# Output group pairs of an attention and SwiGLU kernel: where the sums between the products stand, and in which order the last unit ends

## The chip, the cores and the metric

The kernel runs on one core of a Trainium2 chip. The metric is device time in microseconds (us). A core has five engines with one instruction queue each: TensorE (PE in the profile; its weight loads are listed as PEld), VectorE (DVE), ScalarE (ACT), GpSimd (POOL) and SyncE (SP), which here issues DMAs. Engines meet through semaphores. Each engine takes its own instructions in the order in which the program gives them, so the place of an instruction in that order decides what stands behind it.

## The reference, cut to what matters

```
scores = q @ k^T / sqrt(64)                  # 8 batches x 12 heads, 448 tokens, head width 64
attn   = softmax(scores);  x = attn @ v      # x as 3584 tokens x 768
g, val = x @ w_gate, x @ w_val               # 768 -> 1536
out    = (silu(g) * val) @ w_out             # 1536 -> 768, float32
```

## The kernel before, in words

Tokens are held transposed: features on the 128 partitions, tokens along the free axis. Two batches (896 tokens) make one block of X. Attention for the later heads runs interleaved with the feed-forward part of earlier blocks up to about 301 us. What follows is the tail, and all that the change touches lies in it.

**Products with seven multiplications.** In the tail a 2 x 2 block product is done with seven sub-products in place of eight (the Winograd form). That saves TensorE work and needs sums of operand blocks made ahead: sums of weights (`weight_sums`, L756 to L759, GpSimd, four per unit, called W below), sums of tokens (`token_sums`, L990 to L993, VectorE, tile T), and sums of the hidden values h (`h_sums`, L538 to L541). One call of `h_sums` gives four sums in a chain: s3 = a11 - a21, then a21 becomes a21 + a22 in place, s2 = a21 - a11, s4 = a12 - s2. Each is one instruction over 128 x 768 elements.

**Units.** `Unit` (L793 to L860) computes two feature blocks of g or val for two token halves. There are twelve units, of 256 columns from 301.9 us on (tokens 384 to 895 of the third block), and later twelve of 448 columns (the fourth block). A unit has products P1 to P7 on TensorE (three matmuls each, tiles `un` and `ub`), copies A1 and A2 on ScalarE, sums D1 (L842) and D2 (L846) on VectorE, and four results F00, F01, F10, F11. The results of even units are Silu on ScalarE (L858), those of odd units a multiplication on VectorE (L860) that writes h into `hts`. F11 (the row with `silu,kept`) reads both its operands from SBUF; the other three read one from PSUM. P7 waits for D1 of its unit, P4 for D2.

**The planner.** `order_of` takes items (engine, estimated time, predecessors), runs through them in estimated time, and so fixes the order on every engine. For the units of 256 columns the items hold, beside the units: the W sums of units 6 to 11, then the four G sums (`h_sums` on GpSimd for the first 256 tokens of the third block), four H sums (`h_sums` on VectorE for the tokens 384 to 639; H0 after unit 5, H1 to H3 after unit 11), and the step O: the last `plain_out` (L648), twelve matmuls of 192 columns, one ScalarE copy (L655) and a store of two DMAs on SP. O stands behind P2, P3 and P4 of unit 11.

**Output group pairs.** `out_group` (L677 to L733) gives 256 tokens x 384 output columns with seven products of six matmuls each (0.49 us per product). A pair is two of them, for the two column halves, and shares one set of four h sums. Within a group:

- first stage: products into a, into c (needs the sum a21), into b (needs s2). ScalarE copies a to p1 (L718), VectorE makes p15 (L719) and writes a new c (L721).
- second stage: a product into b again (needs s3); VectorE reads it with the row that the code calls `part` (L725); products into a and into c (needs s4); ScalarE copies the first row out (L696); a third product into b; VectorE reads it (L733). The third product into b may not start before `part` has read b.

`run_groups` runs a pair as: first stage of one, first stage of two, second stage of one, second stage of two. Behind each of these four it takes one instruction from the list `sums` (`add_sum`). So VectorE has four slots for sums per pair, all at the ends of stages. The hook `mid`, called between `part` and the next products, was there already, for another use. Three pairs follow the units of 256 columns (331 to 354 us), and three follow the units of 448 columns (406 us to the end). The slots of the first three hold the T sums for the next units and the h sums of the third pair; four slots are empty. The slots of the last three hold the h sums of the pair that follows.

Of the kernel before, what the change touches and what calls it, by code (L numbers as in the profile page):

```python
# [38 lines left out]
PE_, ACT_, DVE_, POOL_ = "PE", "ACT", "DVE", "POOL"  # L39
# [25 lines left out]
def kernel(  # L65
# [10 lines left out]
    nc = tc.nc  # L76
    B, H, S, D = q.shape
    DM = H * D
    DF = moe_w_gate.shape[1]
    P = 112  # L80
    NC = S // P
    NCB = DM // 128
    NFB = DF // 128
# [53 lines left out]
    NH = NFB // 2  # L137
# [6 lines left out]
    Hall = [[hsum[:, m] for m in range(3)], [hsum[:, 3]]]  # L144
# [5 lines left out]
    def hview(lo, n):  # L150
        return hall[:, ds(lo * NFB, n * NFB)].rearrange("p (f t) -> p f t", t=n)
# [378 lines left out]
            lambda: nc.vector.tensor_sub(t4, b21, t2),  # L530
        ]

    def h_sums(hts, t, at, eng=nc.vector):
        lo, hi, x, y = slice(0, NH), slice(NH, NFB), ts(2 * t, 128), ts(2 * t + 1, 128)
        a11, a12, a21, a22 = hts[:, lo, x], hts[:, hi, x], hts[:, lo, y], hts[:, hi, y]
        s2, s3, s4 = Hall[at]
        return [
            lambda: eng.tensor_sub(s3, a11, a21),  # L538
            lambda: eng.tensor_add(a21, a21, a22),
            lambda: eng.tensor_sub(s2, a21, a11),  # L540
            lambda: eng.tensor_sub(s4, a12, s2),  # L541
        ]
# [339 lines left out]
    with tc.manual_schedule():  # L882
# [48 lines left out]
        sums = []  # L931
# [3 lines left out]
        def pair_groups(kk, c0, hts, t, last=False, at=None):  # L935
            at = t if at is None else at
            osb = []

            def begin(qw, own=False, mid=None):
                if not qw:  # L940
                    osb.extend(new_osb() for _ in range(2))
                return out_group(kk, c0, hts, t, at, qw, osb, last, own, mid)

            return [(lambda own=False, mid=None, qw=qw: begin(qw, own, mid), h_sums(hts, t, at) if not qw else []) for qw in range(2)]
# [41 lines left out]
        def token_sums(x, w, t, eng=nc.vector):  # L986

            b11, b12, b21, b22 = (x[:, ts(h, NK), ts(bb, w)] for h in range(2) for bb in range(2))
            return [
                lambda: eng.tensor_sub(t[0], b12, b11),  # L990
                lambda: eng.tensor_sub(t[1], b22, t[0]),
                lambda: eng.tensor_sub(t[2], b22, b12),
                lambda: eng.tensor_sub(t[3], b21, t[1]),  # L993
            ]
# [14 lines left out]
        def add_sum(n=1):  # L1009
            for _ in range(n):  # L1010
                if sums:
                    sums.pop(0)()
# [149 lines left out]
        while g < last or queue:  # L1162
            n = 2 if g < WIDE * NC else 3
# [33 lines left out]
        for x, (chunks, todo) in enumerate(plan):  # L1197
# [54 lines left out]
            if 0 < base - x <= len(FIRST_STEPS):  # L1252
                n = FIRST_STEPS[x - base]
# [101 lines left out]
        def run_items(items):  # L1355
            items = {n: (e, t, [a for a in after if a in items], fn) for n, (e, t, after, fn) in items.items()}
            for name in order_of(items):
                items[name][3]()

        units = {}  # L1360
        items = unit_items(units, lambda u: Unit(u, 256, x5, t5, hts5), 256)
# [10 lines left out]
        for u in range(6, NFB):  # L1372
            items[f"W_{u}"] = (POOL_, 3.65, [f"W_{u - 1}"], lambda u=u: weight_sums(u))
        groups5 = [pair_groups(KL - 1, 384, hts5, t, at=1 - t) for t in range(2)]
        for m, fn in enumerate(groups5[0][0][1]):
            u = NFB - 1 if m else NH - 1
            items[f"H{m}"] = (DVE_, 0.6, [f"F00_{u}", f"F10_{u}"] + [f"H{m - 1}"] * (m > 0), fn)

        sums.clear()
        for m, fn in enumerate(h_sums(hview(0, 384), 0, 0, nc.gpsimd)):  # L1380
            items[f"G{m}"] = (POOL_, 1.85, [f"G{m - 1}" if m else f"W_{NFB - 1}"], fn)
        items["O"] = (PE_, 1.0, [f"P{n}_{NFB - 1}" for n in (2, 3, 4)], run_o)
        run_items(items)

        def run_groups(pairs):
            for pair in pairs:
                gens = [begin() for begin, _ in pair]
                for stage in range(2):
                    for gen in gens:
                        next(gen)  # L1390
                        add_sum()

        x7 = X[KL]
        t7 = token_space(xp.tile([128, NCB, NT], FP16, tag="X", name="T")[:].rearrange("p a b -> p (a b)"), S)
        tsums7 = token_sums(x7, S, t7)
        behind = groups5[1][0][1]
        rest = lambda: None
        sums.extend([tsums7[0], rest, rest, behind[0], behind[1], behind[2], tsums7[1], behind[3]])
        sums.extend([tsums7[2], rest, rest, tsums7[3]])
        for pair in [groups] + groups5:  # L1400
            run_groups([pair])

        hts = hview(0, NT)
        units = {}
        items = unit_items(units, lambda u: Unit(u, S, x7, t7, hts), S)
# [14 lines left out]
        for m, fn in enumerate(final[0][0][1]):  # L1420
            u = NFB - 1 if m else NH - 1
            items[f"H{m}"] = (DVE_, 0.65, [f"F00_{u}", f"F10_{u}"] + [f"H{m - 1}"] * (m > 0), fn)
        run_items(items)

        sums.extend(f for pair in final[1:] for _, fs in pair for f in fs)
        run_groups(final)


# [28 lines left out]
```

## Time and profile before

| | |
|---|---|
| median of 3 runs | 433.75 us (433.72 to 433.98) |
| profiled execution, its own time | 433.57 us |
| its span in the profile | 431.8 us |
| PE busy | 422.4 us (98%) |
| DVE, ACT, POOL busy | 270.3, 245.5, 233.6 us |
| granted TensorE clock, mean | 0.999 |

The span is counted from the first to the last instruction of the trace; the profiled execution's own time is 1.8 us more. A line of the timeline has the start (us from the start of the span), the duration, the engine, the line of the kernel, the operation, written tile <- read tiles, shape and count. In square brackets stands idle time of that engine before it, and what ended it. Matmuls are pipelined and their ends are modelled: six matmuls of 192 columns show 0.66 us, but the next six start 0.49 us after them. So a stop of TensorE is read from the starts, not from the idle time in the brackets.

### The profile page before, as it was taken

What the parts mean: (1) busy time and instruction counts of PE and PEld (TensorE: products, weight loads), DVE (VectorE), ACT (ScalarE), POOL (GpSimd) and SP (SyncE); (2) the same over time, 40 slices, a digit from 0 to 9 for tenths busy, and PEclk for the clock granted to TensorE, in tenths of its full rate; (3) what the DMA queues carried; (4) which work ended last, traced back from release to release, by engine and by line L of the source; (5) the groups of instructions that cost most, each with busy time, mean ns of one, the idle gap of its engine ahead of it and who ended that gap; (6) DMA issues with size and microseconds to landing.
All of it is one profiled execution on the core that took longest, in us unless ns stands there. A gap on an engine that the chain in (4) does not pass through costs nothing.

```text
span 431.8 us, 11525 instructions
## 1 busy us (share of the span) xinstructions
PE 422.4 (98%) x4594; PEld 286.4 (66%) x4594; DVE 270.3 (63%) x635; ACT 245.5 (57%) x395; POOL 233.6 (54%) x354
## 2 busy tenths in 40 slices
PE   8999999999999999999999999999999999999995
PEld 3666656554557677747665677777888985555795
DVE  4666562775668655575535776677778655565662
ACT  6975667546655655656666546668564225545221
POOL 8756633998877775638744785936997000000001
PEclk9999999999999999999999999999999999999999
DMA  9999999999999999999988998923100231000124
GB/s 141 177 199 200 199 172 182 137 144 226 159 126 138 132 175 124 140 117 133 113 151 127 134 138 109 150 58 84 21 2 25 89 98 49 2 0 2 37 75 147
DMA packets 108550, 50.01 MB, mean 116 GB/s; under 512 B 60864, under 2 KB 105232, under 8 KB 108496
## 3 DMA queue, kind: packets, MB, share of 16 engines
q0 software_dynamic: 46944, 24.83, 52.0%
q1 hardware_dynamic: 61408, 24.27, 32.1%
q8 instruction: 36, 0.59, 0.6%
q10 hardware_dynamic: 144, 0.17, 0.1%
q14 instruction: 18, 0.15, 0.1%
HBM read 49.55 MB, written 11.01 MB: 140 GB/s over the span
## 4 chain that ended last, share of the span: by engine, by line
PE 84%; DVE 7%; DMA 3%; ACT 3%; issue 1%; POOL 1%; SPq 0%; DVEq 0%; POOLq 0%
PE og L677 16%; PE gp L555 15%; PE vp L555 12%; PE un L793 9%; PE acc L418 7%; PE ub L793 7%; PE s L327 4%; PE op L648 3%; PE s L357 2%; PE acc L383 2%; DVE hts L614 2%; DMA qkT<-qk 1%; PE tp L300 1%; DVE t L608 1%; ACT E L347 1%
## 5 line engine op out<-in xcount | busy, mean ns | idle before, releaser
L347 ACT ACTIVATE E<-s 128x896 f16<-128x896 f32 x126 | 106.6, 918 | 40.5 <-PE s L327 28.4
L237 POOL COPY qk<-qkraw 128x512 f16<-128x512 f16 x72 | 44.5, 659 | 55.8 <-DMA qkT<-qk 54.4
L555 PE MATMUL gp<-X,wg 128*128 128x384 f16 (+1 forms) x360 | 73.9, 347 | 0.0
L555 PE MATMUL vp<-X,wv 128*128 128x384 f16 (+3 forms) x360 | 70.1, 332 | 0.2
L608 DVE SCALAR_TENSOR_TENSOR t<-sg,gp 128x384 f32<-128x384 f32 (+1 forms) x60 | 36.3, 607 | 41.6 <-ACT sg L582 41.5
L555 PEld LDWEIGHTS <-wv 128*128 128x128 f16 x420 | 40.3, 98 | 28.1 <-issue 0.6
L638 POOL DMA_DIRECT2D out_dram<-osb x3 | 1.6, 541 | 93.7 <-ACT osb L696 93.7
L555 PEld LDWEIGHTS <-wg 128*128 128x128 f16 x360 | 32.8, 98 | 26.1 <-issue 1.9
L177 POOL DMA_DIRECT2D vraw<-in_v_dram x72 | 43.9, 631 | 9.4 <-DVE t L608 7.1
L582 ACT ACTIVATE sg<-gp 128x384 f32<-128x384 f32 (+1 forms) x60 | 32.1, 537 | 29.2 <-PE gp L555 28.4
L418 PEld LDWEIGHTS <-E 128*128 128x128 f16 (+1 forms) x1152 | 37.3, 96 | 13.1 <-issue 6.8
L177 POOL DMA_DIRECT2D qkraw<-in_k_dram x70 | 42.3, 616 | 6.6 <-DMA wo<-in_moe_w_out_dram 5.3
L677 PEld LDWEIGHTS <-hts 128*128 128x128 f16 x528 | 44.1, 98 | 1.6 <-issue 1.3
L365 ACT ACTIVATE E<-s 112x896 f16<-112x896 f32 x48 | 40.4, 925 | 8.1 <-PE s L357 7.8
L418 PE MATMUL acc<-vo,E 128*128 128x65 f16 (+1 forms) x1152 | 43.3, 193 | 1.4 <-DVE hts L614 0.4
L614 DVE SCALAR_TENSOR_TENSOR hts<-t,vp 128x384 f16<-128x384 f32 (+3 forms) x60 | 34.1, 568 | 7.2 <-PE vp L555 3.3
L696 ACT ACTIVATE osb<-og 128x384 f32<-128x384 f32 x22 | 10.8, 491 | 40.9 <-PE og L677 32.9
L200 POOL DMA_DIRECT2D qkraw<-in_q_dram x44 | 29.8, 678 | 5.7 <-DMA vraw<-in_v_dram 1.4
L448 DVE TENSOR_TENSOR xt<-acc,R 128x256 f16<-128x256 f32 x72 | 30.6, 424 | 2.5
L327 PE MATMUL s<-qkT 64*128 64x448 f16 x216 | 29.6, 353 | 0.0
L677 PE MATMUL og<-wo,hts 128*128 128x192 f16 x264 | 29.0, 246 | 0.0
L677 PEld LDWEIGHTS <-hsum 128*128 128x128 f16 x300 | 25.4, 98 | 1.6 <-DVE og L721 0.6
(180 smaller groups left out, 719.0 us busy)
## 6 DMA issues: line engine op xcount, KB each, us to landing
vraw<-in_v_dram POOLq DMA_DIRECT2D x72, 64.0 KB, 4.8
qkraw<-in_q_dram POOLq DMA_DIRECT2D x41, 112.0 KB, 4.2
qkraw<-in_k_dram POOLq DMA_DIRECT2D x68, 64.0 KB, 4.7
wg<-in_moe_w_gate_dram POOLq DMA_DIRECT2D x8, 288.0 KB, 9.9
wv<-in_moe_w_val_dram POOLq DMA_DIRECT2D x8, 288.0 KB, 10.2
wo<-in_moe_w_out_dram POOLq DMA_DIRECT2D x2, 1152.0 KB, 19.4
out_dram<-osb SPq DMA_DIRECT2D x7, 288.0 KB, 3.6
out_dram<-osb SPq DMA_DIRECT2D x6, 336.0 KB, 3.5
```

The source lines that it names most:

```text
L177: eng.dma_start(dst[ts(s, 64)], rows)
L237: nc.gpsimd.tensor_copy(dst.rearrange("p c h d -> p h c d"), src)
L327: nc.tensor.matmul(s[:, hx, 0:S], lhsT=t[ts(hx, 64), ts(c + low(pr, hx), 128)], rhs=t[ts(hx, 64), ds(NC * 128, S)], start=True, stop=True,)
L347: nc.scalar.activation(e[:, 0 : 2 * S].rearrange("p (h q) -> p h q", h=2), s[:, :, 0:S], AF.Exp, scale=sm_scale)
L365: nc.scalar.activation(e[:, :, 0:S], s[0:P, :, 0:S], AF.Exp, scale=sm_scale)
L418: nc.tensor.matmul(acc[:, ts(j, D + 1)], lhsT=e[rows, ds(hx * S + j * 128, 128)], rhs=Vts[pr % NV][rows, hx, col, 0 : D + 1], start=first, ...
L555: nc.tensor.matmul(dst[:, 0:w], lhsT=wslice(kind, self.fb, cb), rhs=X[kk][:, cb, ds(c0 + lo, w)], start=(cb == 0), stop=(cb == NCB - 1),)
L582: self.readers = [nc.scalar.activation(self.sg[:, 0:n], gp[:, 0:n], AF.Tanh, scale=0.5)]
L608: nc.vector.scalar_tensor_tensor(self.t1[:, 0:n], self.sg[:, 0:n], 1.0, self.gp[:, 0:n], ALU.add, ALU.mult)
L614: nc.vector.scalar_tensor_tensor(self.hts[:, self.fb, ds(lo, w)], self.t1[:, ds(lo, w)], 0.5 * HS, vp[:, 0:w], ALU.mult, ALU.mult)
L677: nc.tensor.matmul(dst, lhsT=lhs(n), rhs=rhs(n), start=first and n == 0, stop=n == NH - 1, skip_group_check=True)
L793: mm = nc.tensor.matmul(dst, lhsT=lhs[:, n], rhs=rhs[:, n], start=first and n == 0, stop=n == NK - 1, skip_group_check=True,)
```

## The change

1. **Slots.** `run_groups` keeps one sum behind the first stage of group one and one behind the whole pair. The two others move into the middle of the second stages (`mid`), between `part` and the last VectorE instruction of the group.
2. **G in halves.** The four GpSimd sums become eight of half the width (three of the six blocks each, 128 x 384), in turn for the two halves.
3. **H behind the units.** The four H sums leave the planner's items. The first is issued straight behind the units, the three others take the next slots. The empty slots are gone; the list is now: T sum 1, H1 to H3 (first pair), the four h sums of the third pair (second pair), T sums 2 to 4 (third pair).
4. **O ahead of P4.** O now stands behind P2, P3 and P7 of unit 11, and P4 of unit 11 behind O.

`run_groups` also runs the last three pairs, so part 1 holds there too.

```
-    def h_sums(hts, t, at, eng=nc.vector):
-        lo, hi, x, y = slice(0, NH), slice(NH, NFB), ts(2 * t, 128), ts(2 * t + 1, 128)
+    def h_sums(hts, t, at, eng=nc.vector, f0=0, n=NH):
+        lo, hi, x, y = ds(f0, n), ds(NH + f0, n), ts(2 * t, 128), ts(2 * t + 1, 128)
         a11, a12, a21, a22 = hts[:, lo, x], hts[:, hi, x], hts[:, lo, y], hts[:, hi, y]
-        s2, s3, s4 = Hall[at]
+        s2, s3, s4 = (h[:, lo] for h in Hall[at])
...
         groups5 = [pair_groups(KL - 1, 384, hts5, t, at=1 - t) for t in range(2)]
-        for m, fn in enumerate(groups5[0][0][1]):
-            u = NFB - 1 if m else NH - 1
-            items[f"H{m}"] = (DVE_, 0.6, [f"F00_{u}", f"F10_{u}"] + [f"H{m - 1}"] * (m > 0), fn)
-
         sums.clear()
-        for m, fn in enumerate(h_sums(hview(0, 384), 0, 0, nc.gpsimd)):
-            items[f"G{m}"] = (POOL_, 1.85, [f"G{m - 1}" if m else f"W_{NFB - 1}"], fn)
-        items["O"] = (PE_, 1.0, [f"P{n}_{NFB - 1}" for n in (2, 3, 4)], run_o)
+        halves = [h_sums(hview(0, 384), 0, 0, nc.gpsimd, f0, NH // 2) for f0 in (0, NH // 2)]
+        for m, fn in enumerate(fn for both in zip(*halves) for fn in both):
+            items[f"G{m}"] = (POOL_, 0.95, [f"G{m - 1}" if m else f"W_{NFB - 1}"], fn)
+        items["O"] = (PE_, 1.0, [f"P{n}_{NFB - 1}" for n in (2, 3, 7)], run_o)
+        items[f"P4_{NFB - 1}"][2].append("O")
         run_items(items)
 
         def run_groups(pairs):
             for pair in pairs:
-                gens = [begin() for begin, _ in pair]
-                for stage in range(2):
-                    for gen in gens:
-                        next(gen)
-                        add_sum()
+                one, two = (begin(mid=add_sum) for begin, _ in pair)
+                next(one)
+                add_sum()
+                for gen in (two, one, two):
+                    next(gen)
+                add_sum()
...
-        behind = groups5[1][0][1]
-        rest = lambda: None
-        sums.extend([tsums7[0], rest, rest, behind[0], behind[1], behind[2], tsums7[1], behind[3]])
-        sums.extend([tsums7[2], rest, rest, tsums7[3]])
+        first, behind = (pair[0][1] for pair in groups5)
+        first[0]()
+        sums.extend([tsums7[0], *first[1:], *behind, *tsums7[1:]])
```

## The prediction

> **What bounds the kernel now.** I read the page first: shares, then the slices.
>
> ```profile
> PE 422.4 (98%) x4594; PEld 286.4 (66%) x4594; DVE 270.3 (63%) x635; ACT 245.5 (57%) x395; POOL 233.6 (54%) x354
> ```
>
> TensorE is the bound and no product is removed, so the change can only win where TensorE stands still. I took the timeline of all engines from 296 us to the end and compared the starts of successive PE rows. Undisturbed, three matmuls of 256 columns take 0.33 us from start to start, six of 192 columns 0.49. Stops of 0.08 us that recur once per two units are left aside. Every larger one, by engine:
>
> ```profile
> 317.89 1.13 DVE L538 TENSOR_TENSOR qkraw<-hts 128x768 f16<-128x768 f16 x1
> 318.81 0.49 PE L793 MATMUL ub<-vraw,E 128*128 128x256 f16 x3
> 318.95 0.41 DVE L846 TENSOR_TENSOR kept<-ub,kept 128x256 f32<-128x256 f32 x1
> 319.41 0.49 PE L793 MATMUL ub<-vraw,wg 128*128 128x256 f16 x3
> ...
> 325.28 1.64 POOL L538 TENSOR_TENSOR hsum<-hts 128x768 f16<-128x768 f16 x1
> 325.82 1.38 DVE L860 SCALAR_TENSOR_TENSOR hts<-silu,kept 128x256 f16<-128x256 f32 x1
> 327.41 0.49 PE L793 MATMUL un<-vraw,vo 128*128 128x256 f16 x3
> 328.26 0.49 PE L793 MATMUL ub<-vraw,wsum 128*128 128x256 f16 x3 [0.36 <-DVE un L842]
> ...
> 330.32 0.49 PE L793 MATMUL un<-X,vo 128*128 128x256 f16 x3
> 331.00 0.49 PE L793 MATMUL ub<-vraw,wv 128*128 128x256 f16 x3 [0.19 <-DVE kept L846]
> 331.05 1.37 DVE L860 SCALAR_TENSOR_TENSOR hts<-silu,kept 128x256 f16<-128x256 f32 x1
> 334.30 0.56 DVE L541 TENSOR_TENSOR qkraw<-hts,hsum 128x768 f16<-128x768 f16 x1
> 334.78 0.35 DVE L719 SCALAR_TENSOR_TENSOR p<-og,p 128x192 f32<-128x192 f32 x1
> 334.79 0.66 PE L677 MATMUL og<-E,hsum 128*128 128x192 f16 x6
> 335.65 0.67 PE L677 MATMUL og<-E,hsum 128*128 128x192 f16 x6 [0.21 <-DVE og L721]
> ```
>
> Read from the starts: P4 of unit 6 is 0.27 late (319.41 - 318.81 - 0.33), behind D2, which stood behind H0. P7 of unit 10 is 0.52 late, behind D1, which stood behind F11 of unit 9. P4 of unit 11 is 0.35 late, behind its own D2. The second stage of the first pair is 0.37 late (335.65 - 334.79 - 0.49): p15 could start only when H3 was through, though ScalarE had p1 ready at 333.83.
>
> The same timeline has the second kind of stop, the third product into b behind `part`:
>
> ```profile
> 343.64 0.55 DVE L540 TENSOR_TENSOR hsum<-hts 128x768 f16<-128x768 f16 x1
> 343.83 0.66 PE L677 MATMUL og<-wo,qkraw 128*128 128x192 f16 x6
> 344.11 0.35 DVE L725 SCALAR_TENSOR_TENSOR osb<-og,p 128x192 f32<-128x192 f32 x1
> 344.51 0.66 PE L677 MATMUL og<-qkraw,hts 128*128 128x192 f16 x6
> ```
>
> A sum goes ahead of `part`; the product starts 0.19 late. By the same reading it is 0.27 late at 346.76, 0.19 at 410.77 and 0.19 at 417.88; in the first pair, where the slot is empty, 0.26 at 337.40, since all of VectorE's work there is late. The third and sixth pair, whose slots there are empty, have no such stop. All nine: 0.27 + 0.52 + 0.35 + 0.37 + 0.26 + 0.19 + 0.27 + 0.19 + 0.19 = 2.61 us.
>
> **H sums behind the units (part 3).** H0 leaves its place at 317.89. D2 of unit 6 then starts when P7 (start 318.15, record 0.49) is through, about 318.66, and ends by 319.08; P4 may start at 319.14 undisturbed. Saved: 0.27. H1 to H3 (three rows of 0.56) leave the stretch ahead of the first p15, and H0 comes there; worked out below.
>
> **G in halves (part 2).** F11 of unit 9 took 1.38 us; its fellows that read PSUM take 0.41. It ended (327.20) 0.28 after the GpSimd sum that ran beside it (326.92). F11 of unit 11 shows the same: end 332.42, GpSimd row to 332.14. So this instruction waits for the GpSimd instruction that is running. A half has the form of the W rows, 128x384, 0.91 us. F11 of unit 9 moves to 325.55 (0.27 earlier), the first half runs from about 325.1 to 326.0, so F11 ends near 326.3 and not 327.2. F01 and F10 follow at 0.34 each, D1 ends near 327.3; P7 of unit 10 is due at 327.47. Saved: 0.52. Bounds: everything if the half ends early, and nothing lost below zero, since a shorter neighbour cannot hold F11 longer; the upper end of its wait is one half plus 0.28, 1.19 us, which still meets P7. GpSimd pays: eight times 0.91 and two extensions of 0.18 (the W rows that run into an F11 show 1.09) give 7.6 us where four took 6.86. It ends near 333.0, not 332.14. Its cover is slack: s2 (sixth half, about 331) is read at 332.2 by the new count, s4 (eighth) at 335.2.
>
> **O ahead of P4 (part 4).** By the planner's rule the order of TensorE changes in this alone. After P3 of unit 11 come the 0.99 us of O, and D2 (0.42) is done inside them. Saved: 0.35. What moves with O: twelve weight loads, the ScalarE copy (0.33; ScalarE was idle 2.34 us before it) and two store DMAs on SP, whose queue is empty from 307 us on. O's bank is that of unit 10, last read at 330.18 minus the 0.79 saved so far: 329.39, before O's start at 329.86. P4 itself comes 0.99 behind its old place in the order, and F10 on VectorE waits for it: P4 ends near 331.35, and F01, which stands ahead of F10, near 331.55, so F10 does not wait.
>
> **The first pair.** TensorE starts it at 332.31 - (0.27 + 0.52 + 0.35) = 331.17. F10 of unit 11 ends near 331.9; the H sum behind it (0.56, up to 1.13 beside GpSimd, as H0 shows) ends between 332.4 and 333.0. The nearest row is H0's: I take 332.5 to 333.0. p1 is ready 1.52 after the pair's start (333.83 - 332.31), 332.7. So p15 starts at 332.75 to 333.0. Before, p15 at 334.78 led through c, T sum 1, the second p15 and c to `part` ending at 337.35, 2.57 later. Now `part` ends at 335.3 to 335.6; the product behind it is due at 331.17 + 9 x 0.494 = 335.62. Both stops (0.37 and 0.26) close, the second with as little as nothing to spare.
>
> **The slots (part 1).** In the second pair `part` starts where the sum stood (343.64) and ends at 344.0, before the 344.33 at which the product is due; likewise for the second group. Saved: 0.19 + 0.27, and 0.19 + 0.19 in the last pairs. Each moved sum now lies between `part` and the last row of the group. That row waits for the third product (0.8 to 1.2 us idle before it on VectorE in all pairs), so a sum of 0.56 or a T sum of 0.86 fits. H2 and H3 of the first pair are read by the second pair's products about 1.4 and 3 us after they end; T sum 2 ends near 348 and is read by P6 at 353.8.
>
> **The sum.** Nothing else is added to TensorE. 433.57 (profiled execution) - 2.61 = 430.96. The median stands 0.18 over that execution, so 431.15 for a median.
>
> One page is weighed. The Trainium skill, SBUF — State Buffer, section Who interferes with whom, says that a VectorE instruction with two SBUF inputs and a GpSimd instruction that reads SBUF exclude each other for a whole instruction, whichever came first. By the rows of F11 the trace agrees, but for about 0.13 us: the second one ends 0.28 after the first and takes 0.41 alone. By that rule H0 in its new place, and no longer after the end of GpSimd's work, is the part that speaks against the change; the rival below prices it.
>
> **The rivals.**
> *Part of the gain only.* H0, now behind the units, meets the last halves. If it waits for the eighth and not the seventh, it ends near 333.4, p15 starts at 333.4, `part` ends at 335.95: 0.3 is kept as a stop, and up to all 0.63 if GpSimd runs later still. For it: H0 took 1.13 at 317.89. Against: VectorE got in after one GpSimd instruction each time. Another source: the chain of waits puts T sum 1 behind a store of O (2.27 us). No idle stands before it on VectorE, so I do not believe it, but if true it waits until 334.1 and costs 0.33. With the 0.63, the 0.33, and 0.3 for F11 beside a half that starts late: 433.75 - 2.61 + 1.26 = 432.4; the middle of this case is 431.9.
> *Slower: the middle sums hold up the products.* They stand in program order ahead of three products. If these waited for the sum, each of two second stages would lose about 1.1 us (344.0 + 0.55 against a product due at 343.34), in five pairs 11 us: 442. It decides from 0.35 us per stage, ten stages, on. Against: an in-place h sum at 409.90 stood ahead of the products at 409.59 and 410.09, and neither waited.
> *No gain: a half costs as much as a whole.* At 1.64 per half s2 would end at 334.9, 2.7 later than its reader at 332.2: 433.75 - 2.61 + 2.7 = 433.8. Against: 0.90 to 0.92 in the undisturbed W rows of that shape. It decides from about 1.1 us per half.
>
> **How the numbers follow.** All nine stops close: 0.60, range 430.7 to 431.6 (the runs shown lie within 0.3). Part of the gain: 0.28, up to 432.6. Middle sums in the way, or any other new wait on that side: 0.07. Halves too dear, within 0.2%: 0.05. 0.2% (0.87 us) is about what a measurement of this kernel can tell from no change. Faster 0.88, same 0.05, slower 0.07. The time is that of the first case, 431.15; the range 430.6 to 432.5 takes in most of the second.
>
> **What would show it.** After: P4 of unit 6 0.33 after the product ahead of it; F11 of unit 9 at 0.5 to 0.9 us; O's rows ahead of the last `ub` rows with no wait; p15 of the first pair started by p1 and not by a sum; `part` in the second, fourth and fifth pair at once behind its product, and six-matmul rows 0.49 apart to the end. The prediction is wrong if a PE row in 331 to 354 us waits for a sum on either engine, or if units 6 to 11 show new stops of D1 or D2.

## The result, and the profile after

The changed kernel takes 430.93 us (median of 6 runs, 430.33 to 431.62), the kernel before 433.87 us (6 runs, 433.57 to 434.66): a ratio of 0.9929, 95% interval 0.9914 to 0.9944. The forecast was 431.15.

The page after, first rows:

```profile
span 429.7 us, 11530 instructions
...
PE 421.5 (98%) x4594; PEld 286.6 (67%) x4594; DVE 267.5 (62%) x635; ACT 245.4 (57%) x395; POOL 234.1 (54%) x358
```

The same 4594 matmuls, and GpSimd has four instructions more (the halves). The shares tell nothing; where the time went has to be read from the starts of the PE rows. This is the timeline of the changed kernel, from the first product of the units to the second pair:

```profile
302.20 0.49 PE L793 MATMUL un<-X,wg 128*128 128x256 f16 x3
...
319.15 0.49 PE L793 MATMUL ub<-vraw,E 128*128 128x256 f16 x3
319.50 0.49 PE L793 MATMUL ub<-vraw,wg 128*128 128x256 f16 x3
...
325.41 1.97 POOL L538 TENSOR_TENSOR hsum<-hts 128x384 f16<-128x384 f16 x2
325.99 0.61 DVE L860 SCALAR_TENSOR_TENSOR hts<-silu,kept 128x256 f16<-128x256 f32 x1
327.57 0.49 PE L793 MATMUL un<-vraw,vo 128*128 128x256 f16 x3
327.90 0.49 PE L793 MATMUL ub<-vraw,wsum 128*128 128x256 f16 x3
...
329.96 0.49 PE L793 MATMUL un<-X,vo 128*128 128x256 f16 x3
330.29 1.15 PE L648 MATMUL op<-wo,hts 128*128 128x192 f16 x12
330.81 1.97 POOL L541 TENSOR_TENSOR hsum<-hts,hsum 128x384 f16<-128x384 f16 x2
331.28 0.49 PE L793 MATMUL ub<-vraw,wv 128*128 128x256 f16 x3
331.61 0.66 PE L677 MATMUL og<-wo,hts 128*128 128x192 f16 x6
331.88 0.42 DVE L860 SCALAR_TENSOR_TENSOR hts<-silu,ub 128x256 f16<-128x256 f32 x1 [0.41 <-ACT osb L655]
332.27 0.92 DVE L538 TENSOR_TENSOR qkraw<-hts 128x768 f16<-128x768 f16 x1
332.80 0.33 ACT L718 ACTIVATE p<-og 128x192 f32<-128x192 f32 x1 [0.99 <-PE og L677]
333.16 0.36 DVE L719 SCALAR_TENSOR_TENSOR p<-og,p 128x192 f32<-128x192 f32 x1
333.90 0.85 DVE L990 TENSOR_TENSOR T<-X 128x1344 f16<-128x1344 f16 x1
335.39 0.35 DVE L725 SCALAR_TENSOR_TENSOR osb<-og,p 128x192 f32<-128x192 f32 x1
335.57 0.66 PE L677 MATMUL og<-wo,hsum 128*128 128x192 f16 x6
336.06 0.66 PE L677 MATMUL og<-qkraw,hts 128*128 128x192 f16 x6
...
342.31 0.35 DVE L725 SCALAR_TENSOR_TENSOR osb<-og,p 128x192 f32<-128x192 f32 x1
342.50 0.66 PE L677 MATMUL og<-wo,qkraw 128*128 128x192 f16 x6
342.58 0.55 DVE L539 TENSOR_TENSOR hts<-hts 128x768 f16<-128x768 f16 x1
342.99 0.66 PE L677 MATMUL og<-qkraw,hts 128*128 128x192 f16 x6
...
424.64 0.66 PE L677 MATMUL og<-qkraw,hts 128*128 128x192 f16 x6
```

What to see: P4 of unit 6 starts 0.35 after the product ahead of it (0.60 before), P7 of unit 10 0.33 after (0.85 before), O follows P3 without a stop and P4 follows O (330.29 + 0.99 = 331.28). In the first pair p15 (333.16) starts 0.03 after p1 is ready (333.13), the same distance as in the trace of parts 1 and 3 together, where VectorE had been waiting for p1 (333.99 and 334.02). The H sum ahead of it has its end at 333.19; rows of VectorE that follow each other without a wait overlap by up to 0.08 (before: H3 to 334.86, p15 from 334.78). So p1 was the last to come, by about 0.05. `part` ends at 335.74, 0.32 before the product that needs b free. In the second pair the in-place sum (342.58) stands behind `part`, and the six-matmul rows are 0.49 apart. None of the nine stops is left.

The whole time is a coarse measure for single parts of the change, since the stretch ahead of the units, which no kernel here changes, ended anywhere from 301.38 to 303.16 us in the traces. So I use the length of the **tail**: from the start of the first product of the 256-column units to the start of the last product of the last pair. It is cut at the first product of the first pair, of the 448-column units, and of the fourth pair. No part changes the 448-column units, and they take 51.94 or 51.95 in all fourteen traces, so differences of a few hundredths of a microsecond can be read from one trace of each kernel:

| trace | units | pairs 1 to 3 | 448-column units | pairs 4 to 6 | tail |
|---|---|---|---|---|---|
| before | 30.45 | 21.87 | 51.95 | 20.66 | 124.93 |
| changed | 29.41 | 20.79 | 51.95 | 20.29 | 122.44 |
| difference | -1.04 | -1.08 | 0.00 | -0.37 | -2.49 |

The two medians differ by 2.94. The 0.45 more would then lie ahead of the units, where the runs scatter; that is worked out, not shown, because only one run of each kernel left a trace. In the experiments with several runs the medians differ from those of the kernel before by between 0.57 less and 0.08 more than the tails do, so 0.45 is of the size of the scatter. In these two traces the units start 0.34 later in the changed kernel, and the two profiled executions are 2.14 apart (433.57 and 431.43): 2.49 less 0.34.

### The profile page after: what moved, and what is told of

The parts are those of the page before. It is cut to its first block, busy times and chain, and to the rows that moved or that the text cites. A ratio compares the mean times of both kernels' runs of the same rounds, so it can differ in the third digit from the quotient of the medians.

```text
span 429.7 us, 11530 instructions
## 1 busy us (share of the span) xinstructions
PE 421.5 (98%) x4594; PEld 286.6 (67%) x4594; DVE 267.5 (62%) x635; ACT 245.4 (57%) x395; POOL 234.1 (54%) x358
## 4 chain that ended last, share of the span: by engine, by line
PE 79%; DMA 12%; DVE 4%; ACT 2%; issue 1%; POOL 0%; SPq 0%; DVEq 0%
PE og L677 17%; PE gp L555 13%; PE un L793 10%; PE vp L555 10%; PE acc L418 8%; PE ub L793 8%; DMA qkraw<-in_k_dram 5%; PE s L327 4%; PE op L648 3%; DMA wv<-in_moe_w_val_dram 3%; DMA vraw<-in_v_dram 3%; PE s L357 2%; DVE hts L614 2%; PE acc L383 1%; ACT E L347 1%
```

## The experiments

Two theories stood against each other. **Stops add up**: each part is worth the stops that it closes, alone or with the others. **Stops are linked**: TensorE must not only come earlier, the instruction it waits for must come earlier as well, and a part that speeds up one side only moves the stop. Each part was made alone on the kernel before, and undone alone in the changed kernel. The measure is the tail.

| kernel | units | pairs 1 to 3 | pairs 4 to 6 | tail | against its base |
|---|---|---|---|---|---|
| before + slots (1) | 30.42 | 21.41 | 20.30 | 124.07 | -0.86 |
| before + halves (2) | 29.91 | 21.77 | 20.67 | 124.30 | -0.63 |
| before + H behind (3) | 30.23 | 21.99 | 20.67 | 124.84 | -0.09 |
| before + O ahead (4) | 30.08 | 22.21 | 20.67 | 124.91 | -0.02 |
| changed without slots | 29.43 | 21.99 | 20.67 | 124.04 | +1.60 |
| changed without halves | 29.85 | 20.79 | 20.30 | 122.89 | +0.45 |
| changed without H behind | 29.57 | 21.71 | 20.30 | 123.52 | +1.08 |
| changed without O ahead | 29.77 | 20.79 | 20.30 | 122.81 | +0.37 |
| before + 1 + 3 | 30.22 | 20.79 | 20.29 | 123.25 | -1.68 |
| before + 2 + 4 | 29.57 | 22.14 | 20.67 | 124.33 | -0.60 |

The four parts alone add to 1.60, the four undone to 3.50, all together give 2.49. So the parts are linked, and the rows show where.

### Slots alone

```
 kernel before, run_groups
-    gens = [begin() for begin, _ in pair]
-    for stage in range(2):
-        for gen in gens:
-            next(gen)
-            add_sum()
+    one, two = (begin(mid=add_sum) for begin, _ in pair)
+    next(one)
+    add_sum()
+    for gen in (two, one, two):
+        next(gen)
+    add_sum()
```

> The kernel before with part 1 alone (two of four sums in the middle of the second stages; the old list, G whole, H in the planner's items, O behind P4). The tail is the time from the start of the first product of the 256-column units to the start of the last product of the last pair: 124.93 before, 122.44 after. Both theories: the stops of 0.19 and 0.27 in the second pair and of 0.19 each in the fourth and fifth pair close, those of the first pair stay: 124.93 - 0.84 = 124.1. If sums in the middle held up products, the tail would be longer than before.

Measured: 124.07; time ratio to the kernel before 0.9986 (0.9975 to 0.9998). The stops of the second, fourth and fifth pair are gone, those of the first pair stand (0.36 and 0.27). Sums in the middle of the second stages cost nothing, so the rival that they hold up products falls.

### Halves alone

```
 kernel before
-    for m, fn in enumerate(h_sums(hview(0, 384), 0, 0, nc.gpsimd)):
-        items[f"G{m}"] = (POOL_, 1.85, ...)
+    halves = [h_sums(hview(0, 384), 0, 0, nc.gpsimd, f0, NH // 2) for f0 in (0, NH // 2)]
+    for m, fn in enumerate(fn for both in zip(*halves) for fn in both):
+        items[f"G{m}"] = (POOL_, 0.95, ...)
```

> The kernel before with part 2 alone (G in halves). Additive theory: only P7 of unit 10 comes on time, 0.52 less: tail 124.4. Theory of linked stops: F11 of unit 11 waits for a half too and not for a whole, so H1 to H3 end 0.6 to 1.2 earlier, and the 0.37 and 0.26 of the first pair shrink or close as well: tail 123.8 to 124.1.

Measured: 124.30; ratio 0.9983 (0.9971 to 0.9995). Here the theory of linked stops named a number that was too low, and the additive one (124.4) came nearer. P7 of unit 10 is on time and F11 of unit 11 takes 0.47, as it said. But H1, which follows, then meets the eighth half. VectorE and GpSimd in the timeline of this kernel:

```profile
330.60 0.47 DVE L860 SCALAR_TENSOR_TENSOR hts<-silu,kept 128x256 f16<-128x256 f32 x1
330.99 0.41 DVE L860 SCALAR_TENSOR_TENSOR hts<-silu,un 128x256 f16<-128x256 f32 x1
331.50 0.42 DVE L860 SCALAR_TENSOR_TENSOR hts<-silu,ub 128x256 f16<-128x256 f32 x1
331.95 1.17 DVE L539 TENSOR_TENSOR hts<-hts 128x768 f16<-128x768 f16 x1
...
334.22 0.35 DVE L719 SCALAR_TENSOR_TENSOR p<-og,p 128x192 f32<-128x192 f32 x1
```

```profile
330.74 1.96 POOL L541 TENSOR_TENSOR hsum<-hts,hsum 128x384 f16<-128x384 f16 x2
```

H1 ends at 333.12, 0.42 after the last half (332.70). Counted from the start of the units (301.95 here, 301.86 before), the first p15 comes 0.65 earlier than before and the pair itself 0.54 earlier, so its two stops stay (0.27 and 0.26, against 0.37 and 0.26). Most of the wait that F11 lost came back at H1.

### H behind the units, alone

```
 kernel before
-    for m, fn in enumerate(groups5[0][0][1]):
-        u = NFB - 1 if m else NH - 1
-        items[f"H{m}"] = (DVE_, 0.6, ...)
...
-    sums.extend([tsums7[0], rest, rest, behind[0], behind[1], behind[2], tsums7[1], behind[3]])
-    sums.extend([tsums7[2], rest, rest, tsums7[3]])
+    first, behind = (pair[0][1] for pair in groups5)
+    first[0]()
+    sums.extend([tsums7[0], *first[1:], *behind, *tsums7[1:]])
```

> The kernel before with part 3 alone: H behind the units and the new list of sums, but all slots at the ends of stages. Additive theory: H0's 0.27 and the first pair's 0.37 and 0.26 close: tail 124.0. Theory of linked stops: H0 is worth 0.2, the 0.37 closes, but every slot now holds a sum ahead of the row that frees b: a stop of about 0.2 in the first pair, 0.2 in the second, 0.5 and 0.25 behind T sums in the third. Tail 124.9 to 125.2, no gain.

Measured: 124.84; ratio 0.9996 (0.9985 to 1.0007). The 0.37 of the first pair closes, the units are 0.22 shorter, and all of it is given back in the pairs: stops of 0.20, 0.20, 0.60 and 0.24, since the list now has a sum for every slot and half of the slots stand ahead of `part`. P7 of unit 10 is 0.46 late here, not 0.52.

### O ahead of P4, alone

```
 kernel before
-    items["O"] = (PE_, 1.0, [f"P{n}_{NFB - 1}" for n in (2, 3, 4)], run_o)
+    items["O"] = (PE_, 1.0, [f"P{n}_{NFB - 1}" for n in (2, 3, 7)], run_o)
+    items[f"P4_{NFB - 1}"][2].append("O")
```

> The kernel before with part 4 alone (O ahead of P4 of unit 11). Additive theory: 0.35 less, tail 124.6. Theory of linked stops: the first pair starts 0.35 earlier, but H1 to H3 end when they did, so its second stage waits 0.35 longer: units 0.35 shorter, the three pairs 0.35 longer, tail 124.9.

Measured: 124.91; ratio 1.0004 (0.9990 to 1.0018). The timeline of this kernel:

```profile
331.75 0.49 PE L793 MATMUL ub<-vraw,wv 128*128 128x256 f16 x3
332.08 0.66 PE L677 MATMUL og<-wo,hts 128*128 128x192 f16 x6
...
334.41 0.56 DVE L541 TENSOR_TENSOR qkraw<-hts,hsum 128x768 f16<-128x768 f16 x1
334.56 0.66 PE L677 MATMUL og<-E,hsum 128*128 128x192 f16 x6
334.89 0.35 DVE L719 SCALAR_TENSOR_TENSOR p<-og,p 128x192 f32<-128x192 f32 x1
335.76 0.67 PE L677 MATMUL og<-E,hsum 128*128 128x192 f16 x6 [0.55 <-DVE og L721]
```

P4 comes right behind O and the units are 0.37 shorter. H3 still ends when it did, so the stop of 0.37 in the first pair is now 0.71 (335.76 - 334.56 - 0.49). Nothing is won: TensorE only came earlier to the same wait.

### The changed kernel without slots

The edit of the first experiment, the other way round, in the changed kernel.

> The changed kernel with part 1 undone: all four slots at the ends of stages, the new list. Additive theory: 0.84 more, tail 123.3. Theory of linked stops: 0.2 in the first pair (H1 ahead of the row that frees b), 0.2 in the second, 0.75 in the third, where T sums 3 and 4 now stand ahead of it, 0.37 in the last pairs: 1.5 more, tail 123.8 to 124.1.

Measured: 124.04; ratio 0.9984 (0.9970 to 0.9998). The third pair in the timeline of this kernel:

```profile
350.44 0.36 DVE L721 SCALAR_TENSOR_TENSOR og<-p,og 128x192 f32<-128x192 f32 x1
350.71 0.85 DVE L992 TENSOR_TENSOR T<-X 128x1344 f16<-128x1344 f16 x1
350.79 0.66 PE L677 MATMUL og<-wo,hsum 128*128 128x192 f16 x6
351.48 0.35 DVE L725 SCALAR_TENSOR_TENSOR osb<-og,p 128x192 f32<-128x192 f32 x1
351.88 0.66 PE L677 MATMUL og<-qkraw,hts 128*128 128x192 f16 x6 [0.43 <-DVE osb L725]
```

T sum 3 stands ahead of `part`, and the product behind `part` is 0.60 late. This pair had no stop in either of the two kernels compared. The slots are worth 0.86 with the old list and 1.60 with the new.

### The changed kernel without halves

```
 changed kernel
-    halves = [h_sums(..., f0, NH // 2) for f0 in (0, NH // 2)]
-    for m, fn in enumerate(fn for both in zip(*halves) for fn in both):
+    for m, fn in enumerate(h_sums(hview(0, 384), 0, 0, nc.gpsimd)):
```

> The changed kernel with part 2 undone: G in four whole sums of 128x768. Both theories: P7 of unit 10 0.5 late again, tail 122.9 to 123.0. The F11 of units 9 and 11 take 1.2 to 1.6 us again. The first pair keeps no stop, since one H sum behind a late F11 still ends in time for the first p15.

Measured: 122.89; ratio 0.9959 (0.9941 to 0.9977). F11 of unit 9 takes 1.28 again, P7 of unit 10 is 0.43 late, and the pairs stay at 20.79. The H sum behind the units starts at 332.26, after the last GpSimd sum (to 331.40), and takes 0.55, where in the changed kernel it takes 0.92 beside the eighth half.

### The changed kernel without H behind the units

The four H items and the old list put back into the changed kernel.

> The changed kernel with part 3 undone: H0 after unit 5 and H1 to H3 after unit 11 on VectorE, the old list with its empty slots. Additive theory: 0.9 more, tail 123.3. Theory of linked stops: H0 0.2; TensorE now comes to the first pair 0.35 and 0.5 earlier than before the change and waits there for H1 to H3, 0.6 and 0.25: 1.0 to 1.1 more, tail 123.4 to 123.6.

Measured: 123.52; ratio 0.9958 (0.9942 to 0.9974). H1 to H3 run to 334.68, the first p15 starts at 334.60, and the first pair stops for 0.65 and 0.26. H1 is not held by a half here (0.56). It starts late, at 332.93, because F10 ahead of it stood idle for 0.76; what held F10 that long is not shown (the profile names the ScalarE copy of O, which was through at 332.06).

### The changed kernel without O ahead

> The changed kernel with part 4 undone: O behind P4 of unit 11. Both theories: P4 waits for D2 again, 0.35 more, tail 122.8. Here the 0.35 shows in full, where part 4 alone is expected to gain nothing by the theory of linked stops.

The edit is that of O alone, the other way round. Measured: 122.81; ratio 0.9947 (0.9926 to 0.9968). P4 is 0.35 late. The same edit that is worth 0.02 on the kernel before is worth 0.37 here, where nothing else holds the first pair.

One row on VectorE is different in this kernel:

```profile
331.70 0.61 DVE L538 TENSOR_TENSOR qkraw<-hts 128x768 f16<-128x768 f16 x1
```

F10 does not wait here, so the H sum starts at 331.70 and gets in between the seventh half and the eighth, whose row then lasts 1.23 from 331.86 on. It ends 1.17 before p1 is ready (333.48). With O ahead of P4, F10 of the changed kernel stands idle for 0.41, the H sum starts at 332.27 and waits for the eighth half. So it is part 4 that moves the H sum behind the last half.

### Two parts at a time

```
 h_and_slots:  kernel before + the edits of parts 1 and 3
 halves_and_o: kernel before + the edits of parts 2 and 4
```

> The kernel before with parts 1 and 3 together, G whole, O behind P4. If each part had a worth of its own, as part 1 alone (0.86) and part 3 alone (0.09) showed: tail 124.93 - 0.95 = 124.0. If the list of part 3 needs the slots of part 1: units 30.2 as with part 3 alone, the three pairs 20.8 and the last three 20.3 as in the changed kernel, tail 123.2 to 123.3.

> The kernel before with parts 2 and 4 together, the old list and slots. If stops add up: 0.35 less than part 2 alone, tail 123.95. If H1 to H3 still hold the first p15, as with part 2 alone (where H1 waited for the eighth half and took 1.17), the 0.35 is given back in the first pair: units 29.6, pairs 22.1, tail 124.3.

Measured: 123.25 and 124.33 (one execution each). Parts 1 and 3 together close every stop in the pairs (20.79 and 20.29, as in the changed kernel), 1.68 where their sum alone is 0.95. On top of them halves and O add their full worth: 1.68 + 0.45 + 0.37 = 2.50, and the change measures 2.49. Parts 2 and 4 together give 0.60, no more than the halves alone: the units end 0.88 earlier, and the first pair, which still waits for H1 to H3, is 0.27 longer. The cause is not quite the expected one: H1 takes 0.56 and not 1.17, but starts only at 332.67, since F10 ahead of it stood idle for 0.74, as in the changed kernel without H behind the units.

### G in sixths

```
 changed kernel
-    halves = [h_sums(..., f0, NH // 2) for f0 in (0, NH // 2)]
+    halves = [h_sums(..., f0, 1) for f0 in range(NH)]
```

> The changed kernel with the G sums in sixths, 24 instructions of 128x128 and not 8 of 128x384. From 1.64 for 768 and 0.91 for 384, an estimate of a fixed 0.18 and 0.24 per block gives 0.42 for each, 10.1 in all, so G ends near 335.5 by the trace of the changed kernel and s4 still comes about in time for its reader at 335.6: tail 122.4 to 122.9. If a small instruction cost about as much as a half (0.91), G would take 22 and the first pair would wait for s2 and s4: tail over 128.

Measured: 122.62 (one execution). GpSimd in the timeline of this kernel:

```profile
324.99 2.54 POOL L538 TENSOR_TENSOR hsum<-hts 128x128 f16<-128x128 f16 x6
327.48 2.35 POOL L539 TENSOR_TENSOR hts<-hts 128x128 f16<-128x128 f16 x6
329.78 2.91 POOL L540 TENSOR_TENSOR hsum<-hts 128x128 f16<-128x128 f16 x6
332.65 2.97 POOL L541 TENSOR_TENSOR hsum<-hts,hsum 128x128 f16<-128x128 f16 x6
```

TensorE, the product that reads s2 and the one behind it:

```profile
332.18 0.83 PE L677 MATMUL og<-E,hsum 128*128 128x192 f16 x6
332.84 0.66 PE L677 MATMUL og<-wo,hts 128*128 128x192 f16 x6
```

About 0.4 for each, as estimated, and G ends at 335.62. F11 of unit 9 takes still less (0.52), but that buys nothing, since P7 was already on time. The cost shows: 0.17 in the first pair (332.84 - 332.18 - 0.49), at the product that reads s2, which is done at 332.69. So the halves cost no TensorE time only because G has room behind them, and this is about where the room ends. The rival of a dear half falls.

### P1 ahead of P7

```
 changed kernel, run_items, for the 256-column units and odd u from 1 to 9
+    names.remove(f"P1_{u + 1}")
+    names.insert(names.index(f"P7_{u}"), f"P1_{u + 1}")
```

> The changed kernel, and P1 of the next even unit ahead of P7 of each odd unit 1 to 9, the rest of every order as it was. What is left in the tail is a stop of 0.08 per two units before P7 of the odd unit, which waits for D1. If a third product between P6 and P7 covers it and P4 behind it still has its D2 in time: 0.06 to 0.08 less for each of five, tail 122.1. If the stop only moves to P4: tail 122.4.

Measured: 122.21; 430.59 us (6 runs, 430.17 to 432.03), ratio to the kernel before 0.9940 (0.9923 to 0.9956). Units 29.18, 0.23 less than in the changed kernel; of the six stops of 0.08 before P7 only that of unit 11 is left, where there is no next P1. A little comes back elsewhere: P4 of the odd units is now 0.02 to 0.03 late, and one product 0.06. The H sum behind the units takes 1.16 here, and p15 starts 0.22 after p1 is ready (332.44, 332.22) and not 0.03. `part` still ends at 335.00, 0.15 before the product behind it, and the pairs stay at 20.79. By the tail this version beats both kernels; the whole times of the two do not separate them.

## Why the prediction was right, point by point

- **The bound and the measure.** TensorE stood still at nine places, and closing them gives the time. Forecast 2.61, measured 2.49 in the tail. Of the 0.12 between them, 0.08 is the small stop named in the next point; the rest is spread over several terms in hundredths. The medians moved by 2.94, and what goes beyond the tail is not foreseen by the prediction.
- **H0 (0.27).** Mis-sized. The units are 0.22 shorter with part 3 alone and 0.16 longer with it undone. Unit 7 of the kernel before lacks the stop of 0.08 ahead of P7 that every other odd unit shows; its P7 (320.06) comes two products behind the late P4 of unit 6 (319.41), so part of H0's cost was paid back at once. I had set those small stops aside as constant.
- **Halves (0.52).** Measured 0.45 (undone), F11 of unit 9 at 0.61 inside the forecast 0.5 to 0.9. A part of the 0.52 goes with part 3, since the stop is 0.46 with part 3 alone. GpSimd's work lasts from 325.41 to 332.78, 7.4 against an estimate of 7.6. One bound does not hold by the prediction's own rows: an F11 of 1.19 from 325.55 on would end at 326.74, D1 about 1.0 later, near 327.7, and P7 is due at 327.47. It did not come to that.
- **O ahead (0.35).** Measured 0.37, given the other parts. Alone it is worth 0.02. The prediction had its cover right but spoke of "saved" without saying that the saving stands only once H1 to H3 are out of the way. One step of it failed: F10 does wait, 0.41, though the prediction says that it does not. P4 is through at 331.77 and the ScalarE copy of O at 331.81, F10 starts at 331.88; the profile names the copy, and which of the two held it is not shown. F01 ahead of F10 ended earlier than forecast (331.47; less the 0.34 by which this trace is later, 331.13 against 331.55). F10 ended where the forecast had it (332.30, less 0.34, against 331.9).
- **The first pair (0.37 + 0.26).** Closed, and the times are those of the forecast: p15 at 333.16, less 0.34, is 332.82 (forecast 332.75 to 333.0), and the end of `part` 335.40 (335.3 to 335.6). The way there was another. The H sum took 0.92: it came while the eighth half ran, waited for it and ended 0.41 after it. That is the premise of the rival "part of the gain only". It did no harm because GpSimd was through at 332.78, less 0.34 at 332.44, where the forecast had 333.0. That p15 still came at the forecast time is in part luck. `part` had 0.32 to spare, where I had counted on as little as nothing; with P1 ahead of P7 the H sum took 1.16, p15 came 0.19 late, and there was still no stop. The Trainium skill (SBUF — State Buffer, Who interferes with whom) says that a VectorE instruction with two SBUF inputs contends with a GpSimd instruction that reads SBUF. The trace agrees but for a small overlap: the H sum takes 0.56 alone and ends 0.41 after the GpSimd sum, so 0.15 of it overlaps.
- **A store ahead of T sum 1.** The chain's reading falls. T sum 1 started at 333.90, as soon as VectorE was free, while the two stores of O, issued from 331.84 on, landed 3.2 and 3.4 after issue.
- **The slots (0.46 and 0.38).** Measured 0.46 in the second pair with part 1 alone, and 0.36 and 0.37 in the last three. The last row of each group did not become late for anyone.
- **The rivals on the other side.** No PE row in the pairs waits for a sum, and a half costs 0.9; both are excluded by rows of the changed kernel. (The price of the first one, about 1.1 per stage, is 1.2 by the numbers given there: 344.0 + 0.55 - 343.34. Nothing rests on it.)

## What to carry to other kernels

A stop of the bounding engine has two sides: what makes that engine early and what makes its partner late. Before pricing an edit alone, ask which wait ends second; O ahead was worth 0.02 or 0.37 by that alone. When sums are put into slots between dependent products, the place relative to the instruction that frees a PSUM bank matters more than the number of sums, and a fuller list needs the better slots first.

## What the runs showed that I had not expected

Splitting the GpSimd sums shortens the wait of the VectorE instruction beside the early ones, but GpSimd ends later (30.75 after the start of the units with halves alone, 30.28 before), and the next VectorE sum with two SBUF operands met the late end: H1 took 1.17 in place of 0.56. Moving O ahead of P4 delayed F10 and with it the H sum, which then met that late end in the changed kernel. And the stretch ahead of the units, the same instructions in all fourteen traces, ends between 301.38 and 303.16 us; that spread of 1.8 us is larger than any single part of this change. What causes it was not tried. A lower granted clock it is not: the mean over the span is 1.000 in the trace that comes to 303.16, and 0.999 in the one that comes to 301.38.
